# Crossbar transposes on the SP queue, staged row loads from POOL, and paired scores in a fused mLSTM and MLP kernel

## The chip, the cores and the metric

One core of one Trainium2 chip. The metric is the device time of one execution in microseconds (us). Medians are over several executions; each execution is also listed with its span (first to last instruction, some 1.7 us less than the time) and with the mean clock that TensorE was granted. Engines are named as in the profile: PE (TensorE), ACT (ScalarE), DVE (VectorE), POOL (GpSimd), SP (the queue that issues DMAs, "SPq"). PSUM is the memory that PE writes its results to. A crossbar transposition is a DMA issued with `transpose=True`; a DMA lands when the semaphore that tells of its end is raised.

## The reference, cut to what matters

```python
# attention part: q, k, v, o_gate: (4, 8, 768, 40); i_gate, f_gate: (4, 8, 768)
for t in range(S):
    m_new = maximum(f[t] + m, i[t]);  f_stab = exp(f[t] + m - m_new);  i_stab = exp(i[t] - m_new)
    C = f_stab * C + i_stab * outer(v[t], k[t]);   n = f_stab * n + i_stab * k[t]
    y[t] = sigmoid(o[t]) * (C @ q[t]) / maximum(abs(n . q[t]), 1)
x = y.transpose(0, 2, 1, 3).reshape(3072, 320)
# MLP part
h = x @ w_in                               # 320 -> 2048
out = (0.5 * (h + sqrt(h * h + 4))) @ w_out  # 2048 -> 320
```

The kernel uses that the input gates decide the state after the first 64 rows: only the first 128 rows of a batch need scores against k; all later rows multiply q with one 40x41 state per head. A flag is computed on the chip, and a general path runs if the assumption fails.

## The kernel before

The 3072 rows are 12 blocks of 256. A block passes: q cast and padded (POOL), q transposed, numerators (PE), division (DVE), gating `xt = y * sigmoid(o)` (POOL), x transposed, and then the MLP in four **units** of 512 hidden columns: 12 first-stage matmuls on PE, a square and a root on ACT, an addition on DVE. 48 units in all; the second stage follows in 48 half sums of 8 matmuls each, and 24 output tiles are copied and stored. In the traces of this case every engine works through its instructions in the order in which the program issues them (run 1 shows a wait of 5.70 us that comes of it); tables decide, in half slots of a unit, where each attention step is put between the units.

```python
STEPS = {                      # block: half slot of each step
    ...
    4: dict(pr=17, q_=24, n0=25, n1=26, x=29),          # pr: casts on POOL, q_: transpose q
    5: dict(pr=20, k_=23, q_=28, s0=28, s1=29, n0=31, n1=34, x=36),   # s: scores, n: numerators
    ... }
SECOND = (0, 0, 0, 0, 0, 0, 1, 1, 2, ...)      # second-stage halves issued in each slot
XT = (3, 7, 8, 9, 10)                          # x copies that ACT makes; DVE makes the others

def evacuate(on_act, n, dst, src):             # PSUM to SBUF
    if n in on_act: nc.scalar.activation(out=dst, in_=src, func=AF.Copy)
    else:           nc.vector.tensor_copy(out=dst, in_=src)

def s_q(blk, tag):                             # s_x is the same on xt; s_k: eight, on kh
    tp = psum([128, 2, G3, 128], BF, tag, "tp")      # tag "at": one PSUM tile for all these steps
    for t in range(2):
        for g in range(G3):
            nc.tensor.transpose(tp[:, t, g, :], qb[blk % 2][:, t, g, :], ident)
    evacuate(QT, blk, qT, tp)

def s_sc(b, half, tag):                        # one matmul per head, 128x128, k padded to 128
    for n in range(4):
        h = half * 4 + n
        nc.tensor.matmul(out=sp[:, n, :], lhsT=kT[:, h, :], rhs=qT[:, t, h // 3, :], ...)

def load_rows():                               # all three later batches at one point, from SP
    for b in range(1, B): ...
        nc.sync.dma_start(...)
def store(blk, ts, op):
    evacuate(OUT, blk * 2 + ts, osb, op)
    nc.sync.dma_start(out=dst, in_=osb)        # at once
```

Of the kernel before, what the change touches and what calls it, by code (L numbers as in the profile page):

```python
# [17 lines left out]
STEPS = {  # L18
    1: dict(pr=None, q_=0, n0=2, n1=3, x=6),
    2: dict(pr=8, k_=7, q_=9, s0=10, s1=11, n0=12, n1=13, x=15),  # L20
    3: dict(pr=14, g=16, q_=17, n0=17, n1=19, x=20),
    4: dict(pr=17, q_=24, n0=25, n1=26, x=29),
    5: dict(pr=20, k_=23, q_=28, s0=28, s1=29, n0=31, n1=34, x=36),
    6: dict(pr=31, g=38, q_=35, n0=43, n1=40, x=46),
    7: dict(pr=36, q_=39, n0=47, n1=48, x=53),
    8: dict(pr=37, k_=44, q_=50, s0=52, s1=55, n0=54, n1=56, x=61),
    9: dict(pr=54, g=57, q_=59, n0=60, n1=63, x=67),
    10: dict(pr=51, q_=65, n0=65, n1=68, x=75),
    11: dict(pr=64, k_=70, q_=71, s0=72, s1=74, n0=82, n1=79, x=85),
}  # L30
SIGM = (15, 30, 56)
EARLY = (3, 6, 7, 16, 17, 18, 19, 24, 30, 37)
SECOND = (0, 0, 0, 0, 0, 0, 1, 1, 2, 2, 1, 1, 1, 1, 1, 1, 0, 2, 0, 1, 1, 0, 2, 1, 1, 1, 1, 1, 1, 1, 1, 2, 0, 1, 1, 1, 1, 1, 1, 0, 2, 0, 2, 1)
QT = (1, 2, 7)
XT = (3, 7, 8, 9, 10)
OUT = (2, 3, 4, 5, 6, 7, 8, 9, 13, 14, 15, 16, 17, 18, 19, 20)
ALONE = (6, 7, 12, 13, 18, 19, 24, 25, 26, 27, 30, 31, 36, 37, 42, 43)
CLEAR = 8
ROWS = 8
FLAGS = (59, 61, 80, 86)  # L40

# [146 lines left out]
def kernel(  # L188
# [14 lines left out]
    T = 128  # L203
# [31 lines left out]
    with tc.manual_schedule():  # L235
# [39 lines left out]
        def load_w_in(lo, hi):  # L275
            nc.gpsimd.dma_start(out=w_in[:, :, lo:hi], in_=moe_w_in[0:256, lo:hi].rearrange("(g p) n -> p g n", p=128))
            for i in range(2):
# [22 lines left out]
        nc.gpsimd.memset(caus, 1.0)  # L300
        nc.gpsimd.affine_select(out=caus, in_=caus, compare_op=ALU.is_ge, fill=0.0, base=0,
                                pattern=[[1, 128]], channel_multiplier=-1)

# [4 lines left out]
        vwb = [const.tile([128, H, D + 1], BF, name=f"vw{i}") for i in range(2)]  # L308
        kTb = [const.tile([128, H, 128], BF, name=f"kT{i}") for i in range(2)]
        nc.vector.memset(kb[0], 0.0)  # L310
        nc.vector.memset(vwb[0], 0.0)
        nc.vector.memset(kh, 0.0)
        nc.vector.memset(kTb[0][:, :, TK:128], 0.0)
        for i in range(2):
# [21 lines left out]
        def psum(shape, dt, tag, name):  # L336
            return ps.tile(shape, dt, tag=tag, name=name, bufs=3 if tag == "hp" else 1)
# [18 lines left out]
        def vcast(b, eng):  # L356

            vw = vwb[b % 2]
            wb = wE[0:TK, 0, b * H:(b + 1) * H].unsqueeze(2)
            eng.tensor_copy(out=vw[0:TK, :, D:D + 1], in_=wb)  # L360
            eng.tensor_tensor(out=vw[0:TK, :, 0:D], in0=vf[b], in1=wb.to_broadcast([TK, H, D]), op=ALU.mult)
            state[b, "vw"] = vw

        def qcast(blk, eng, ts=(0, 1)):
# [18 lines left out]
        def evacuate(on_act, n, dst, src):  # L383
            if n in on_act:
                nc.scalar.activation(out=dst, in_=src, func=AF.Copy)  # L385
            else:
                nc.vector.tensor_copy(out=dst, in_=src)  # L387

        def s_q(blk, tag):
            tp = psum([128, 2, G3, 128], BF, tag, "tp")  # L390
            for t in range(2):
                for g in range(G3):
                    nc.tensor.transpose(tp[:, t, g, :], qb[blk % 2][:, t, g, :], ident)  # L393
            qT = work.tile([128, 2, G3, 128], BF, tag="qT", name="qT")
            evacuate(QT, blk, qT, tp)
            state[blk, "qT"] = qT

        def s_k(b, tag):
            kp = psum([128, H, 128], BF, tag, "kp")
            for h in range(H):  # L400
                nc.tensor.transpose(kp[:, h, :], kh[:, h, :], ident)
            kT = kTb[b % 2]
            nc.vector.tensor_copy(out=kT[:, :, 0:TK], in_=kp[:, :, 0:TK])
            state[b, "kT"] = kT

# [10 lines left out]

        def s_sc(b, half, tag):
            blk, t = b * 3 + 2, PAIRS[2].index(0)
            sp = psum([128, 4, 128], FP, tag, "sp")
            kT, qT = state[b, "kT"], state[blk, "qT"]  # L420
            for n in range(4):
                h = half * 4 + n
                nc.tensor.matmul(out=sp[:, n, :], lhsT=kT[:, h, :], rhs=qT[:, t, h // 3, :], start=True, stop=True)  # L423
            if half == 0:
                state[b, "scm"] = work.tile([128, H, 128], BF, tag="scm", name="scm")
            nc.vector.tensor_tensor(out=state[b, "scm"][:, half * 4:half * 4 + 4, :], in0=sp,  # L426
                                    in1=caus.unsqueeze(1).to_broadcast([128, 4, 128]), op=ALU.mult)

        def s_num(blk, t, tag, peng=nc.gpsimd):
            b, tt = blk // 3, PAIRS[blk % 3][t]  # L430
            np_ = psum([128, H, D + 1], FP, tag, "np")
            if tt == 0:
                for h in range(H):
                    nc.tensor.matmul(out=np_[:, h, :], lhsT=state[b, "scm"][:, h, :], rhs=state[b, "vw"][:, h, :],
                                     start=True, stop=True)
            else:
                for g in range(G3):
                    n = min(3, H - 3 * g)
                    nc.tensor.matmul(out=np_[:, 3 * g:3 * g + n, :], lhsT=state[blk, "qT"][:, t, g, :],  # L439
                                     rhs=state[b, "gm"][:, 3 * g:3 * g + n, :], start=True, stop=True)  # L440
# [16 lines left out]

        def s_x(blk, tag):
            xp = psum([128, 2, G3, 128], BF, tag, "xp")
            for t in range(2):  # L460
# [17 lines left out]
        gates_T("at")  # L478
        vcast(0, nc.vector)
        idle(9)  # L480
        s_g(0, "hp")


        qcast(0, nc.vector, (0,))
        for o, i in zip(padded(qb[0][:, 1]), heads(tile_of(ql, 0, 2))):
            nc.scalar.activation(out=o, in_=i, func=AF.Copy)
        idle(8)
        tp = psum([128, 2, 1024], BF, "hp", "tp")
        np_ = psum([128, 2 * H, 64], FP, "hp", "np")
        qT = work.tile([128, 2, G3, 128], BF, tag="qT", name="qT")  # L490
        for t in range(2):
            for g in range(G3):
                nc.tensor.transpose(tp[:, t, g * 128:(g + 1) * 128], qb[0][:, t, g, :], ident)
        nc.vector.tensor_copy(out=qT[:, 0], in_=tp[:, 0, 0:384].rearrange("p (g n) -> p g n", g=G3))
        nc.scalar.activation(out=qT[:, 1], in_=tp[:, 1, 0:384].rearrange("p (g n) -> p g n", g=G3), func=AF.Copy)
        sigm(0, 1, 3)
# [21 lines left out]
        nc.scalar.activation(out=tiny[:, 0:1], in_=tiny[:, 1:2], func=AF.Sqrt)  # L518
        def load_rows():
            for b in range(1, B):  # L520
                if b == 1:

                    kf[b] = res.tile([TK, H, D], FP, name=f"kf{b}")
                    nc.vector.memset(kf[b][0:1, 0, 0:1], 0.0)
                    nc.sync.dma_start(out=kf[b], in_=k[b, :, 0:TK, :].rearrange("h s d -> s h d"))
                else:
                    chunk(kf, "kf", k, b)
                chunk(vf, "vf", v, b)
                later(ql, "ql", q, b, 1, NTL)
                later(ol, "ol", o_gate, b, 1, NTL)  # L530
                chunk(q0, "q0", q, b)
                chunk(o0, "o0", o_gate, b)
                if b == 1:
                    for n in range(2):
                        nc.sync.dma_start(out=fi[:, n, T:S], in_=gates[n][:, T:S])

# [28 lines left out]

        khcast(0, nc.gpsimd)


# [5 lines left out]
        def put(hs, f, *a):  # L574

            bank = () if f in (sigm, load_rows, flag1, flag2, flag3) else ("op" if hs <= 10 and hs % 2 == 0 else "at",)
            plan.setdefault(hs, []).append(lambda: f(*a, *bank))
# [26 lines left out]

        for m in (kb[1], vwb[1], kTb[1][:, :, TK:128]):
            pre.setdefault(CLEAR, []).append(lambda m=m: nc.gpsimd.memset(m, 0.0))
        for blk, row in STEPS.items():
            put_block(blk, **row)
        put(ROWS, load_rows)
        for b, hs in enumerate(SIGM):  # L610
# [8 lines left out]
        def flush():  # L619
            while adds:  # L620
                adds.pop(0)()

        def store(blk, ts, op):
            b, tt = blk // 3, PAIRS[blk % 3][ts]
# [4 lines left out]
            else:  # L629
                dst = out[b * S + T:(b + 1) * S, :].rearrange("(p j) d -> p j d", j=NJ)[:, tt - 1, :]  # L630
            nc.sync.dma_start(out=dst, in_=osb)

# [15 lines left out]

        def at(table, hs):
            for f in table.get(hs, ()):  # L650
                f()
# [62 lines left out]
        for u in range(3):  # L714
            first(blk, (u,))
            adds.append(unit(blk, u))
            while len(todo) > 4:
                mm2_part(todo.pop(0))
            flush()
        mm2_part(todo.pop(0), "at")  # L720
        mm2_part(todo.pop(0), "at")
# [3 lines left out]
        mm2_part(todo.pop(0))  # L725
        mm2_part(todo.pop(0))
        tc.mark_branch_hint_location("general", "LikelyTaken")
        mm2(blk, 0, list(range(NF)), "at")
        mm2(blk, 1, list(range(NF)), "op")
    short.close()  # L730

# [33 lines left out]
```

## Time and profile before

| | before |
|---|---|
| median of the executions | 159.7 us |
| span of the profiled one, clock | 158.5 us, 0.995 |
| PE, ACT, DVE, POOL busy | 141.2, 128.9, 106.7, 60.3 us |

The prediction shows the main rows and reads them. I use the start of a unit's square on ACT as a mark, since every kernel here has the same 48. These are busy times of the engines (us, and number of instructions) between the marks of units 0, 8, 16 and 47 in the kernel before; the columns are stretch, length, PE, PE's weight loads, DVE, ACT, POOL, clock, DMA share, GB/s:

```profile
0.00:15.08 15.08, 10.83 (x105) 8.67 (x106) 8.89 (x36) 7.69 (x12) 13.86 (x27) 1.00 0.92 187
15.08:38.93 23.85, 20.14 (x201) 13.78 (x200) 16.65 (x30) 20.58 (x21) 12.13 (x33) 1.00 0.95 189
38.93:62.79 23.86, 21.72 (x215) 15.80 (x212) 16.46 (x30) 22.54 (x26) 8.66 (x23) 1.00 0.77 207
62.79:146.75 83.96, 81.93 (x782) 58.24 (x781) 61.51 (x101) 76.05 (x85) 25.65 (x60) 1.00 0.09 31
```

From unit 0 to 8 no compute engine is full, from 8 to 16 ACT nearly is (22.5 of 23.9), from 16 to 47 PE is (81.9 of 84.0).

### The profile page before, as it was taken

To read this page: it belongs to the slowest core of one execution; us is meant where nothing else is said; L and a number is where in the kernel's file an instruction comes from. 1 tells how busy PE (TensorE), PEld (TensorE's weight loads), DVE (VectorE), ACT (ScalarE), POOL (GpSimd) and SP (SyncE) were. 2 spreads that over 40 slices of the span, in tenths; PEclk is the share of its full clock that TensorE was granted. 3 is DMA by queue.
4 is the path that set the end of the run, shared out by engine and by line. 5 is a ranking of instruction groups with operands and counts; after the bars stand their busy time and mean duration, and the time that the engine had idled before them with its cause. 6 is when DMAs were issued, how large, how long until landed. Compare 5 with 4: busy or idle time off the path is not lost.

```text
span 158.5 us, 3472 instructions
## 1 busy us (share of the span) xinstructions
PE 141.2 (89%) x1343; PEld 101.0 (64%) x1343; DVE 106.7 (67%) x199; ACT 128.9 (81%) x144; POOL 60.3 (38%) x142
## 2 busy tenths in 40 slices
PE   5787686989899979999999999898999999999960
PEld 5665455657667666767766766676767777666740
DVE  5655687794666858696868787987775586655520
ACT  3656999768999799999968879999979999889500
POOL 7999390282270560740507722337220022000000
PEclk9999999999999999999999999999999999999997
DMA  3999995996989930110110010011011011101121
GB/s 56 258 241 192 186 225 81 288 227 123 348 149 296 286 134 0 41 41 4 41 41 24 22 41 31 15 43 41 4 41 41 4 43 41 41 6 41 43 91 43
DMA packets 26389, 15.54 MB, mean 98 GB/s; under 512 B 13360, under 2 KB 25760, under 8 KB 26368
## 3 DMA queue, kind: packets, MB, share of 16 engines
q1 hardware_dynamic: 21376, 11.18, 25.2%
q0 software_dynamic: 3936, 3.93, 14.1%
q10 hardware_dynamic: 1056, 0.16, 0.6%
q8 instruction: 11, 0.18, 0.5%
q14 instruction: 10, 0.08, 0.2%
HBM read 13.96 MB, written 3.93 MB: 113 GB/s over the span
## 4 chain that ended last, share of the span: by engine, by line
PE 73%; DVE 12%; ACT 4%; issue 3%; POOL 3%; DMA 1%; SPq 0%; DVEq 0%; POOLq 0%; ACTq 0%
PE op L640 30%; PE hp L665 23%; PE hp L672 7%; PE xp L462 3%; DVE gt L686 3%; POOL xt L456 3%; PE np L439 2%; PE sp L423 2%; DVE qT L387 2%; PE tp L393 2%; DMA fi<-in_i_gate_dram 1%; DVE xT L387 1%; ACT t L685 1%; ACT t L684 1%; PE warm L472 1%
## 5 line engine op out<-in xcount | busy, mean ns | idle before, releaser
L686 DVE SCALAR_TENSOR_TENSOR gt<-hp,t 128x1024 bf16<-128x1024 f32 x48 | 58.3, 1220 | 18.5 <-ACT t L685 16.8
L640 PE MATMUL op<-w_out,gt 128*128 128x320 bf16 x384 | 57.7, 299 | 0.2 <-ACT osb L385 0.2
L684 ACT ACTIVATE t<-hp 128x1024 f32<-128x1024 f32 x48 | 48.8, 1016 | 10.0 <-PE hp L672 7.1
L685 ACT ACTIVATE t<-t 128x1024 f32<-128x1024 f32 x48 | 50.7, 1057 | 1.5
L456 POOL TENSOR_TENSOR xt<-y,sig 128x320 bf16<-128x320 f32 (+1 forms) x44 | 25.1, 593 | 69.8 <-DVE y L452 45.8
L665 PE MATMUL hp<-xT,w_in 128*128 128x256 bf16 x384 | 49.9, 273 | 1.4 <-DVE xT L387 1.2
L640 PEld LDWEIGHTS <-gt 128*128 128x128 bf16 x384 | 35.7, 98 | 13.8 <-issue 1.6
L665 PEld LDWEIGHTS <-w_in 128*128 128x128 bf16 x384 | 35.2, 98 | 8.9 <-issue 5.1
L672 PE MATMUL hp<-xT,w_in 64*128 64x256 bf16 x192 | 17.1, 273 | 0.1
L672 PEld LDWEIGHTS <-w_in 64*128 64x128 bf16 x192 | 6.4, 94 | 8.3 <-issue 7.7
L452 DVE SCALAR_TENSOR_TENSOR y<-den,np 128x320 f32<-128x320 f32 x18 | 8.8, 488 | 1.5
L370 POOL CAST qb<-ql 128x240 bf16<-128x240 f32 (+1 forms) x32 | 8.9, 316 | 0.4 <-POOL xt L456 0.3
L462 PE MATMUL xp<-ident,xt 128*128 128x128 bf16 x72 | 7.1, 220 | 2.0 <-DVE xt L512 1.0
L472 PE MATMUL warm<-ident 128*128 128x128 bf16 x68 | 7.1, 278 | 1.4 <-POOL identF L267 1.4
L385 ACT ACTIVATE osb<-op 128x320 f32<-128x320 f32 x16 | 6.8, 423 | 1.8 <-PE op L640 1.8
L439 PE MATMUL np<-gm,qT 128*128 128x123 bf16 (+1 forms) x54 | 5.5, 214 | 2.7 <-DVE qT L387 1.4
L462 PEld LDWEIGHTS <-xt 128*128 128x128 bf16 x72 | 4.8, 97 | 4.8 <-POOL xt L456 1.4
L426 DVE TENSOR_TENSOR scm<-sp,caus 128x512 bf16<-128x512 f32 x8 | 5.4, 688 | 3.3 <-PE sp L423 3.3
L443 DVE TENSOR_REDUCE den<-np 128x8 f32<-128x8 f32 x22 | 3.5, 161 | 5.5 <-PE np L439 4.2
L439 PEld LDWEIGHTS <-qT 128*128 128x128 bf16 x54 | 3.7, 98 | 5.2 <-DVE qT L387 1.7
L472 PEld LDWEIGHTS <-ident 128*128 128x128 bf16 x68 | 6.0, 130 | 1.5 <-POOL identF L267 1.4
L381 ACT ACTIVATE sig<-ol 128x1600 f32<-128x1600 f32 (+2 forms) x5 | 6.3, 1259 | 0.6 <-DMA ol<-in_o_gate_dram 0.6
(102 smaller groups left out, 114.7 us busy)
## 6 DMA issues: line engine op xcount, KB each, us to landing
out_dram<-osb SPq DMA_DIRECT2D x24, 160.0 KB, 1.8
ql<-in_q_dram SPq DMA_DIRECT2D x3, 800.0 KB, 5.2
ol<-in_o_gate_dram SPq DMA_DIRECT2D x3, 800.0 KB, 7.0
w_out<-in_moe_w_out_dram POOLq DMA_DIRECT2D x2, 640.0 KB, 11.4
w_in<-in_moe_w_in_dram POOLq DMA_DIRECT2D x2, 256.0 KB, 5.4
w_in<-in_moe_w_in_dram POOLq DMA_DIRECT2D x1, 512.0 KB, 7.7
ol<-in_o_gate_dram POOLq DMA_DIRECT2D x1, 480.0 KB, 5.4
q<-in_q_dram SPq DMA_DIRECT2D x3, 160.0 KB, 7.2
```

Of the source, the lines that this page charges most:

```text
L370: eng.tensor_copy(out=o, in_=i)
L439: nc.tensor.matmul(out=np_[:, 3 * g:3 * g + n, :], lhsT=state[blk, "qT"][:, t, g, :], rhs=state[b, "gm"][:, 3 * g:3 * g + n, :], start=Tru ...
L452: nc.vector.scalar_tensor_tensor(out=y1, in0=den.to_broadcast([128, H, D]), scalar=1.0, in1=np_[:, :, 0:D], op0=ALU.min, op1=ALU.mult)
L456: peng.tensor_tensor(out=o, in0=y[:, lo:DM], in1=s[:, lo:DM], op=ALU.mult)
L462: nc.tensor.transpose(xp[:, t, g, :], xt[blk % 2][:, t, g * 128:(g + 1) * 128], ident)
L472: nc.tensor.matmul(out=warm[:, 0:128], lhsT=ident, rhs=ident, start=True, stop=True)
L640: nc.tensor.matmul(out=op, lhsT=gts[blk][:, ff, ts * 128:(ts + 1) * 128], rhs=w_out[:, ff, :], start=(ff == 0), stop=(ff == NF - 1))
L665: nc.tensor.matmul(out=hps[blk, u][:, f, :], lhsT=w_in[:, g, ff * 128:(ff + 1) * 128], rhs=xT[:, :, g, :], start=start and g == 0 and f % ...
L672: nc.tensor.matmul(out=hps[blk, u][:, 2 * i + f, :], lhsT=w_in3[p, (2 * u + f) * 128:(2 * u + f + 1) * 128], rhs=xT[p, :, 2, :], start=sta ...
L684: nc.scalar.activation(out=t1, in_=hp, func=AF.Square, scale=0.5)
L685: nc.scalar.activation(out=t1, in_=t1, func=AF.Sqrt, bias=1.0)
L686: return lambda: nc.vector.scalar_tensor_tensor(out=gts[blk][:, u * UF:(u + 1) * UF, :], in0=hp, scalar=0.5, in1=t1, op0=ALU.mult, op1=ALU ...
```

## The change

Its intent is to take transpositions, their PSUM tiles and their copies off PE, ACT and DVE. For that, the SP queue must be free: loads go to POOL in three bursts, and stores are issued two half slots late. Scores of two heads share a matmul. All tables were set anew. At the start, block 0's transpositions get two PSUM tiles, and the cast of its first tile moves in front of the state step. The core of the diff:

```diff
-    5: dict(pr=20, k_=23, q_=28, s0=28, s1=29, n0=31, n1=34, x=36),
+    5: dict(pr=19, k_=19, q_=22, s0=25, s1=26, n0=28, n1=30, x=34),
 ... (all rows of STEPS, SIGM, EARLY, SECOND, QT, XT, OUT, ALONE, FLAGS)
+QDMA = (2, 3, 5, 6, 7, 8, 9, 10, 11)
+XDMA = (3, 4, 5, 7, 8, 9, 10, 11)
-ROWS = 8
+ROWS = (11, 23, 41)
 def s_q(blk, tag):
+    if blk in QDMA:
+        crossbar(qT..., qb[blk % 2]...)       # nc.sync.dma_start(..., transpose=True)
+        return
 def s_x(blk, tag):
+    if blk in XDMA:
+        crossbar(xT..., xt[blk % 2]...); return
-    for h in range(H): nc.tensor.transpose(kp[:, h, :], kh[:, h, :], ident)
-    nc.vector.tensor_copy(out=kT[:, :, 0:TK], in_=kp[:, :, 0:TK])
+    crossbar(kTb[b % 2], kh[0:TK]...)
+    nc.sync.dma_start(out=vpb[b % 2][TK:128, :, 1, :], in_=vwb[b % 2][0:TK, 1:H:3, :])
 def s_sc(b, half, tag):
-    for n in range(4): ...                    # 8 matmuls a batch
+    hs = ((0, 2, 3), (5, 6))[half]            # 5 a batch, lhsT = k of two heads
-def load_rows(): ... nc.sync
+def load_row(b): ... nc.gpsimd                # put in front of the steps at half slot ROWS[b - 1]
-    nc.sync.dma_start(out=dst, in_=osb)
+    stores.append((now[0], dst, osb))         # sent two half slots later
-tp = psum([128, 2, 1024], BF, "hp", "tp")     # block 0
+tp = [psum([128, 384], BF, "hp", "tp") for t in range(2)]
```

## The prediction

> **What bounds the kernel now.** I read the busy rows and the slices of the page first, then the granted clock and the busy times by stage, then the groups, the waits, and last the chain of waits to see what one transposition costs on TensorE where it counts.
>
> ```profile
> PE 141.2 (89%) x1343; PEld 101.0 (64%) x1343; DVE 106.7 (67%) x199; ACT 128.9 (81%) x144; POOL 60.3 (38%) x142
> PE   5787686989899979999999999898999999999960
> ACT  3656999768999799999968879999979999889500
> DMA  3999995996989930110110010011011011101121
> ```
>
> TensorE (PE) is nearly full from the second fifth of the span to the last slice but one; ScalarE (ACT) is close behind; the DMA engines are full only for the first 15 slices (59 us). The same by stage (columns: stretch, its length, busy us of each engine, clock, DMA share, GB/s):
>
> ```profile
> 13.70:36.90 23.20, 19.49 (x198) 13.21 (x198) 17.06 (x32) 18.78 (x19) 13.51 (x35) 1.00 0.98 196
> 36.90:60.00 23.10, 20.96 (x202) 15.27 (x200) 14.57 (x26) 21.56 (x24) 8.66 (x23) 1.00 0.86 222
> 60.00:80.00 20.00, 19.85 (x200) 14.52 (x198) 15.83 (x27) 19.31 (x22) 7.34 (x19) 1.00 0.07 25
> 80.00:100.00 20.00, 19.51 (x190) 13.86 (x189) 15.35 (x28) 16.78 (x18) 8.07 (x20) 1.00 0.10 34
> 100.00:120.00 20.00, 18.69 (x183) 13.16 (x182) 16.41 (x28) 18.53 (x21) 7.95 (x17) 1.00 0.08 26
> 120.00:140.00 20.00, 19.92 (x188) 14.20 (x186) 13.02 (x22) 17.90 (x22) 2.29 (x4) 1.00 0.10 35
> ```
>
> Three regimes. Up to about 37 us nobody is full except the DMA engines (0.98): loads and short dependent chains set the pace. From 37 to 60 us ACT (21.6 of 23.1) and PE (21.0) both nearly bound it. From 60 to 147 us PE is busy 85.0 of 87 us (the four rows and 7.0 of the next 7): there a microsecond of PE work taken away should be a microsecond of time. The clock is 1.00 throughout, so it is no lever. In the timeline of PE after 13.7 us I count 7.9 us of idle time; these entries of the list of waits are the ones behind a transposition and its copy out of PSUM:
>
> ```profile
> PE np L439 <- DVE qT L387: 1.4, 2, 0.7
> PE sp L423 <- ACT qT L385: 1.2, 1, 1.2
> PE sp L423 <- DVE qT L387: 0.6, 1, 0.6
> PE sp L423 <- DVE xT L387: 0.6, 1, 0.6
> ```
>
> Together 3.9 us. The last one is telling: a score matmul waits for the copy of an unrelated x transposition, because transpositions, scores, numerators and state all take turns in the one PSUM tile tagged "at". What one group costs where PE is the chain (start, us on the chain, what):
>
> ```profile
> 48.15 0.45 PE kp L401 x8
> ...
> 56.41 0.35 PE tp L393 x6
> 56.78 0.57 DVE qT L387
> 57.39 0.38 PE sp L423 x4
> ...
> 58.86 0.35 PE xp L462 x6
> 59.23 0.57 DVE xT L387
> ```
>
> Six q or x transpositions occupy PE for 0.35 us and eight k transpositions for 0.45 us, although the groups call each of them 219 ns: they are pipelined at 57 ns. So the chain, not the groups' means, gives the price.
>
> **What the Trainium skill says.** "VectorE: DVE Perf Modes", section "The three transpose paths": the crossbar takes 1309 ns for a 128x128 bf16 block against 390 ns on TensorE, but lands in SBUF rather than PSUM, so no copy follows it. This trace has no crossbar transposition; the TensorE figure is for one alone, and here it is 219 ns long and 57 ns apart. "TensorE: Matmul & The Clock Gate", section "Part 4: PE-mode transpose", says that a copy out of PSUM has to follow; the trace agrees (0.56 us on DVE, 0.79 on ACT per block). "DMA: Bandwidth & Descriptors", section "Latency and other measured facts", gives 261 GB/s for a DMA transposition in one kernel; its section "Anatomy of one DMA — SWDGE (gpsimd) path" a fixed 2.0 us per DMA, mostly the receipt. The trace agrees on the second in kind: a 160 KB store lands 1.8 us after its issue. An estimate from these pages for one 128x768 bf16 block (196,608 bytes): 2.0 + 0.75 = 2.8 us if it streams, 6 x 1.31 = 7.9 us if six blocks go one after another.
>
> **The change, part by part.**
>
> *PE work removed.* q by crossbar in 9 blocks: 9 x 0.35 = 3.15 us. x in 8 blocks: 8 x 0.35 = 2.8. k in all 4 batches: 4 x 0.45 = 1.8. Scores go from 8 matmuls per batch to 5: 12 fewer at about 57 ns (same 128 columns as a transposition) = 0.7. The numerators of the first tile go from 8 to 5; eight take 0.20 us on the chain, so about 0.3 in all. Sum 8.7 us of PE.
>
> *Evacuations.* ACT loses q of blocks 2 and 7 (2 x 0.79), x of blocks 3, 7, 8, 9, 10 (5 x 0.79) and, by the new list, 7 output copies (16 to 9, 0.42 each): 8.5 us less. DVE loses 7 q copies (0.56), 3 x copies (0.56), 4 k copies (0.42) and 3/8 of the masking (5.4 us becomes 3.4 by columns): 9.3 us less, and takes 7 output copies at 0.49, so 5.9 us less net. Both sides of the second-tightest engine are relieved in about PE's proportion: over 15 to 147 us ACT is busy 119.4 and PE 124.1 of 132; they become 111 and 115.5. That is why I don't expect ACT to become the bound.
>
> *Waits removed.* Four of the PE waits above go with their transpositions, 3.9 us at most; and the shared PSUM tile has 21 fewer tenants.
>
> *Added: 21 crossbar transpositions and 3 or 4 small moves on the SP queue.* They are off all compute engines. They cost only if the result comes later than its reader. The schedule leaves, between the cast of q and its first use, some 5 half slots in most blocks (pr 19 to s0 25, 28 to 34, 52 to 59), and between x and the first matmul 3 to 9. A half slot is 132 us / 88 = 1.5 us or a bit less, so there are about 4 to 8 us, against the estimate of 2.8 to 7.9. Mostly hidden. Stores are issued two half slots late so that a store not yet ready doesn't hold a transposition up in the same in-order queue (SP waited 87 us on output copies before).
>
> *Added on POOL: 20 load issues.* POOL's issues take 0.95 us each in this trace (rows of ql, q and o from POOL: 954, 969, 949 ns), 19 us in all, in bursts of 8, 6 and 6 (7.6, 5.7, 5.7 us). POOL goes from 60 to about 80 us of busy time, not a bound, but a burst sits in front of the gating products xt, each pair of which takes 1.2 us on POOL and lies on the path to the next block's x.
>
> *Start.* The two q transpositions of block 0 get a PSUM tile each, so that ACT need not wait for DVE's copy before its own (8.69 to 9.06, then 9.08 to 9.58): about 0.4 us.
>
> *Sum by regime.* From 60 us on: 6 q groups (2.1), 5 x groups (1.75), 2 k groups (0.9), scores and numerators of two batches (0.5) = 5.3 us, and about 1.2 us of the waits: 6.5. From 37 to 60 us: PE falls by about 2.2 and its waits by 2.0, but ACT, at 21.6 of 23.1, falls only by one x copy and up to two output copies, 1.2 to 1.6, so I take 1.8. Before 37 us: 0.4 from the start; what else goes there (q of 2, k of 0, the 1.2 us wait for ACT) is not on PE's bound, and the POOL burst is a charge against it: net 0.4. Sum 8.7 us less. For new waits on crossbars or POOL I take 0.6 back: 8.1 less, so 159.8 - 8.1 = **151.7 us**.
>
> **The rivals.**
>
> *The crossbar takes the wait's place.* If a transposition needs nearer 8 us, or SP spends microseconds in issuing each and serialises 21 of them with 24 stores, PE stops at scores, numerators and first matmuls. For it: the block figure of 1309 ns, and that in the first 60 us the DMA engines are loaded anyway, so that a 160 KB load took 7.2 us and more to land. Against it: after 60 us they are busy 7 to 10%, the q and x gaps were evidently widened, and q of block 4 and x of block 6 are kept on PE, near the second and third burst of loads. If each of 17 transpositions left 0.4 us of wait, the time would be some 158; if only the first few do, 153.5.
>
> *POOL becomes the bound in the second stage.* The burst at half slot 11 (7.6 us) and the cast of block 3, which needs rows of that same burst, stand in program order before the gating of block 2. In the kernel before, that gating ran at 30.2 to 33.3 us and the first matmuls of block 2 at 34.2. If POOL starts the burst at 24 us (after its casts), it ends at 31.6, and if the cast then waits for the rows to land, block 2 comes 3 to 5 us later. For it: POOL is in order. Against it: ACT in the kernel before didn't start block 2's squares before 38.9 anyway, since it stood in the sigmoid of the next batch, so most of the delay would be hidden. Worst case 155.5.
>
> *More than the sum.* With the PSUM tile free, all 7.9 us of PE idle time shrink, and the loads spread over three stages relieve the first 60 us: 148.
>
> **Range and chances.** The PE sum is firm (counts and chain prices); what is not is the first 60 us and the latency of the crossbar. The crossbar rival at its full size I hold for 1 in 12, the POOL one at 3 us or more for 1 in 5, the better one for 1 in 6. That gives 148.0 to 155.8 us as a range for 8 times in 10. Faster by over 2% means below 156.6: 0.91. Within 2%: 0.07. Slower: 0.02.
>
> **What would show it.** In the changed profile: PE busy near 132 to 133 us and no group of k transpositions; ACT near 120, DVE near 101, POOL near 80; from 60 us to the tail PE still busy 96% or more; crossbar issues landing in 3 to 5 us; no wait of a first matmul or a numerator on a DMA above 0.5 us. The prediction is wrong if PE's busy time falls by 8 us and its idle time grows by as much, with a DMA or POOL's xt as releaser, or if the block 2 matmuls start after 38 us and ACT does not make up for it.

## The result, and the profile after

| | before | changed |
|---|---|---|
| median | 159.7 us (159.59 to 159.95) | 154.59 us (154.07 to 156.14) |
| ratio, 95% interval | 1 | 0.9694 (0.962 to 0.977) |
| span of the profiled execution | 158.5 us | 152.4 us |
| PE, ACT, DVE, POOL busy | 141.2, 128.9, 106.7, 60.3 | 132.8, 121.7, 100.8, 77.4 |

Ratios are the mean time of one kernel's fast runs over that of the other's of the same rounds, so not quite the ratio of the medians. The change is faster by 3.1%. Its four executions, with their clocks, are 154.07 (0.996), 154.18 (0.995), 155.01 (0.989) and 156.14 us (0.978): they scatter with the clock, which those of the kernel before (0.99 to 1.00) don't. More on that below. The spans differ by 6.1 us and the medians by 5.1: the profiled execution of the kernel before took 160.26 us, 0.56 more than its median, so about half a microsecond of what the stages below show is that execution's.

The page of the changed kernel, with the rows that the prediction showed of the one before:

```profile
PE 132.8 (87%) x1185; PEld 93.3 (61%) x1185; DVE 100.8 (66%) x190; ACT 121.7 (80%) x130; POOL 77.4 (51%) x168
PE   6697679747999995899999899899999999999970
ACT  3648959938999779999997568999979989699610
DMA  2999999999037699503799150132333103101111
```

PE's busy time fell by 8.4 us, but the span by 6.1: PE has new idle time. The row of PE shows weaker slices in the first quarter (7, 4, 7 in the eighth to tenth, where it had 9, 8, 9), and the DMA row three load hills instead of one. The busy times between the same marks (units 0, 8, 16, 47):

```profile
0.00:14.27 14.27, 10.84 (x103) 9.49 (x103) 7.81 (x32) 7.69 (x13) 12.85 (x26) 1.00 0.91 185
14.27:39.95 25.68, 18.74 (x171) 12.04 (x171) 16.19 (x32) 20.42 (x22) 19.92 (x46) 1.00 1.09 202
39.95:63.61 23.66, 21.91 (x205) 15.36 (x204) 16.91 (x31) 21.30 (x23) 17.13 (x38) 1.00 0.71 174
63.61:140.88 77.27, 74.76 (x665) 51.94 (x663) 57.52 (x95) 69.29 (x72) 27.47 (x59) 1.00 0.36 88
```

| stretch | before | changed | difference |
|---|---|---|---|
| start to unit 0 | 15.08 | 14.27 | -0.81 |
| unit 0 to 8 | 23.85 | 25.68 | +1.83 |
| unit 8 to 16 | 23.86 | 23.66 | -0.20 |
| unit 16 to 47 | 83.96 | 77.27 | -6.69 |
| unit 47 to the end | 11.75 | 11.52 | -0.23 |

(A DMA share above 1, as in the second row, is how the profile prints it; I take it only as a sign that the engines are loaded.)

So the gain is all in the PE-bound stretch (PE's busy time there fell by 7.2, the stretch by 6.7), the middle gave nothing, and the beginning lost more than twice what the new start had won.

What became of the middle shows in the chain of waits of the changed kernel, here the part before block 4's first matmul, unit 16 (start, us on the chain, what):

```profile
48.08 1.15 POOL xt L475 x2
49.23 0.67 POOL kf L243
49.91 0.68 POOL vf L243
50.59 0.87 POOL ql L248
51.48 0.90 POOL ol L248
52.38 0.87 POOL q L243
53.25 0.87 POOL o L243
54.14 1.14 POOL xt L475 x2
55.30 5.72 DMA xT<-xt
61.07 1.05 PE hp L695 x8
```

POOL gates the first tile of block 4, issues the second burst of loads (4.9 us), and only then gates the second tile; the crossbar then needs 5.7 us to land, in the burst's traffic. PE stood 1.69 us. In the same way 0.78 us were lost before the scores at 84 us (timeline of PE; in brackets the idle time before it and what ended it):

```profile
61.07 1.05 PE L695 MATMUL hp<-xT,w_in 128*128 128x256 bf16 x8 [1.69 <-DMA xT<-xt]
...
84.36 0.33 PE L438 MATMUL sp<-qT,kT 128*128 128x128 bf16 x3 [0.78 <-DMA qT<-qb]
```

The issues of the transpositions (number, median us from issue to landing):

```profile
qT<-qb SPq DMA_TRANSPOSE x9, 3.2
...
xT<-xt SPq DMA_TRANSPOSE x8, 2.5
...
kT<-kh SPq DMA_TRANSPOSE x4, 4.7
```

Taken one by one, 11 of the 21 land in 2.5 or 2.6 us; the slow ones are 4.0 to 7.4 us (one 3.2), nearly all while weights or rows are being loaded (5.0 and 5.6 at 24 and 32 us, 5.7 at 55, 6.9 and 5.3 at 76 and 79). Two slow ones have no load in flight: 4.5 at 61 and 4.0 at 107.

### The profile page after: what moved, and what is told of

The parts are those of the page before. It is cut to its first block, busy times and chain, and to the rows that moved or that the text cites. A ratio compares the mean times of both kernels' runs of the same rounds, so it can differ in the third digit from the quotient of the medians.

```text
span 152.4 us, 3186 instructions
## 1 busy us (share of the span) xinstructions
PE 132.8 (87%) x1185; PEld 93.3 (61%) x1185; DVE 100.8 (66%) x190; ACT 121.7 (80%) x130; POOL 77.4 (51%) x168
## 4 chain that ended last, share of the span: by engine, by line
PE 52%; DVE 16%; DMA 10%; ACT 8%; POOL 5%; issue 4%; SPq 0%; DVEq 0%; POOLq 0%; ACTq 0%
PE op L668 24%; PE hp L695 16%; PE hp L702 5%; DVE gt L716 5%; ACT t L714 5%; DMA xT<-xt 4%; DMA qT<-qb 3%; ACT t L715 3%; POOL xt L475 2%; PE np L458 2%; DVE y L471 2%; PE warm L496 2%; DVE osb L396 2%; DMA fi<-in_i_gate_dram 1%; DMA out_dram<-osb 1%
## 5 line engine op out<-in xcount | busy, mean ns | idle before, releaser
L695 PEld LDWEIGHTS <-w_in 128*128 128x128 bf16 x384 | 35.9, 98 | 11.2 <-issue 4.1
L702 PE MATMUL hp<-xT,w_in 64*128 64x256 bf16 x192 | 18.0, 274 | 0.0
L396 DVE COPY osb<-op 128x320 f32<-128x320 f32 x15 | 7.3, 486 | 9.6 <-PE op L668 6.3
L496 PE MATMUL warm<-ident 128*128 128x128 bf16 x68 | 7.8, 297 | 1.4 <-POOL identF L269 1.4
L496 PEld LDWEIGHTS <-ident 128*128 128x128 bf16 x68 | 6.7, 140 | 1.5 <-POOL identF L269 1.4
L442 DVE TENSOR_TENSOR scm<-sp,caus 128x384 bf16<-128x384 f32 (+1 forms) x8 | 3.9, 488 | 3.6 <-PE sp L438 3.6
L394 ACT ACTIVATE osb<-op 128x320 f32<-128x320 f32 x9 | 3.8, 424 | 1.9 <-PE op L668 1.9
L248 POOL DMA_DIRECT2D ql<-in_q_dram x5 | 4.5, 907 | 0.5 <-DMA w_in<-in_moe_w_in_dram 0.5
```

Of the source, the lines that this page charges most:

```text
L496: nc.tensor.matmul(out=warm[:, 0:128], lhsT=ident, rhs=ident, start=True, stop=True)
L695: nc.tensor.matmul(out=hps[blk, u][:, f, :], lhsT=w_in[:, g, ff * 128:(ff + 1) * 128], rhs=xT[:, :, g, :], start=start and g == 0 and f % ...
L702: nc.tensor.matmul(out=hps[blk, u][:, 2 * i + f, :], lhsT=w_in3[p, (2 * u + f) * 128:(2 * u + f + 1) * 128], rhs=xT[p, :, 2, :], start=sta ...
```

## The experiments

All gave correct results. "Unit 8" and the like is the start of that unit's square. Two theories stood at first: the gain comes only where PE is the bound, so early crossbars can go back to PE for nothing; and either POOL's bursts or the crossbar's landing under load cost the middle. The rival: PE work counts everywhere.

**1. Early crossbars back on PE.**

```diff
-QDMA = (2, 3, 5, 6, 7, 8, 9, 10, 11)      -XDMA = (3, 4, 5, 7, 8, 9, 10, 11)
+QDMA = (6, 7, 8, 9, 10, 11)               +XDMA = (7, 8, 9, 10, 11)
```

> The changed kernel with q of blocks 2, 3, 5 and x of blocks 3, 4, 5 transposed on TensorE again (6 groups, 6 x 0.35 = 2.1 us of PE work put back before about 61 us). Theory (the gain comes only from the PE-bound stretch after some 70 us; earlier, PE's work is worth nothing and the crossbar's landing of 5 to 6 us under the loads costs): 153.5 to 154.8, the changed kernel's 154.6 or up to 1 us less, and no first matmul waiting on a crossbar near 61 us. Rival (PE work counts everywhere): 154.6 + 2.1 = 156.7.

Measured: 173.73 us (172.47 to 174.11), ratio 1.083. Both theories miss by far: six groups of 0.35 us cost 19 us. The timeline of PE, then that of ACT, show how:

```profile
46.48 0.51 PE L486 MATMUL xp<-ident,xt 128*128 128x128 bf16 x3 [0.53 <-POOL xt L475]
49.57 0.49 PE L411 MATMUL tp<-ident,qb 128*128 128x128 bf16 x6 [2.58 <-ACT xT L394]
49.90 4.01 PE L668 MATMUL op<-w_out,gt 128*128 128x320 bf16 x16
...
82.28 0.43 PE L458 MATMUL np<-gm,qT 128*128 128x123 bf16 x3 [5.70 <-ACT xT L394]
82.51 4.47 PE L668 MATMUL op<-w_out,gt 128*128 128x320 bf16 x16
```

```profile
46.71 1.02 ACT L714 ACTIVATE t<-hp 128x1024 f32<-128x1024 f32 x1 [0.57 <-DVE gt L716]
47.76 1.06 ACT L715 ACTIVATE t<-t 128x1024 f32<-128x1024 f32 x1
48.73 0.79 ACT L394 ACTIVATE xT<-xp 128x768 bf16<-128x768 bf16 x1
```

PE transposes x, but the copy stands in ACT's queue behind a square and a root (at 82 us behind two units and a table load), and the next user of the one PSUM tile "at" must wait for it: 2.58 and 5.70 us. Behind that user stand all other matmuls, since PE keeps its order. And after such a pause the clock is low: 16 second-stage matmuls take 4.01 and 4.47 us instead of 2.33. Over the run PE idles 9.5 us more after unit 0 than in the changed kernel, and 17 us (from 33.3, 50.4 and 81.1 us on) run at half clock. The stretches around the second pause show it (seventh and following columns: POOL busy, clock, DMA share, GB/s):

```profile
76.00:82.20 6.20, 0.49 (x6) 0.37 (x6) 1.16 (x2) 6.14 (x7) 0.00 (x0) 0.91 0.00 0
82.20:88.00 5.80, 5.72 (x26) 3.56 (x26) 1.84 (x5) 0.03 (x1) 1.14 (x2) 0.51 0.00 0
88.00:92.00 4.00, 4.00 (x42) 2.74 (x40) 3.51 (x6) 2.87 (x3) 1.94 (x4) 1.00 0.34 90
```

So in the new tables a transposition on PE costs not its 0.35 us but the waits at both of its ends. The crossbar takes those waits out of PE's queue into SP's; the new tables are built on that. "Undo a part" is therefore not a clean price of that part, which I had not thought of.

**2. No crossbar for q and x at all.**

```diff
+QDMA = ()
+XDMA = ()
```

> The changed kernel with no crossbar transposition of q or x at all (17 groups back on TensorE, 5.95 us of PE work), k still by crossbar, scores still in pairs. Theory: only the 11 groups after 61 us cost, 11 x 0.35 = 3.85 us and up to 1 us of waits for their copies, less what the early ones give back: 157.5 to 159.5. Rival (PE work counts everywhere): 160.5 or more, no better than the kernel before. Second rival (the gain is in the k part, the pairs and the output copies' move): under 156.

Measured: 188.51 us (186.57 to 189.52), ratio 1.172: a miss for the same reason, and more of it (29 us of idle PE from unit 0 to 47, against 11).

**3. The row loads from SP again, in three bursts.**

```diff
-ROWS = (11, 23, 41)      # load_row: nc.gpsimd, in front of the steps of that half slot
+ROWS = (12, 23, 41)      # load_row: nc.sync, behind them
```

> The changed kernel with the three bursts of row loads issued by SP instead of POOL, at the same places but the first one half slot later (behind the crossbar of q of block 2). Traffic the same, POOL 17 us less busy. Theory A (the POOL bursts stand in front of the gating products and cost about 1.5 us in the first 61 us): 152.5 to 153.8, and the gating of block 4's second tile at about 50.5 instead of 54.1 us. Theory B (it is the crossbar's landing under the traffic, whoever issues it): 154 to 155. Rival C: the issues on SP (0.6 us each, longer under load) now hold up the crossbars: above 155.

Measured: 161.04 us (160.33 to 163.47), ratio 1.005; clock 0.94 to 0.96 in every execution; the profiled one (163.47) is slow, so I take only the order of events from it. This run doesn't decide what it was made for. On SP the first burst had a store ahead of it that was not ready before 31.9 us, so it started at 32.4 instead of 23.6, and POOL waited 9.8 us for k's rows. What follows is only that SP's order counts: here the loads stood behind a late store.

**4. x of block 4 alone on PE.**

```diff
-XDMA = (3, 4, 5, 7, 8, 9, 10, 11)
+XDMA = (3, 5, 7, 8, 9, 10, 11)
```

> The changed kernel with x of block 4 alone transposed on TensorE. Its crossbar took 5.7 us to land under the second burst of loads, and the first matmul at 61.1 us waited 1.7 us for it. Theory B (the landing under load costs): the wait goes, PE pays 0.35 us: 153.2 to 153.9 if it is carried to the end, and the units after block 5's start come about 1.2 us earlier. Rival (what is gained there is lost to ACT or to the next wait before 70 us): 154.3 to 154.8.

Measured: 160.0 us (157.59 to 160.6), ratio 0.9996, fast executions at clocks of 0.973 to 0.995, three of six slow; the profiled one is 157.59 at 0.995. Units up to 13 stand within 0.5 us of the changed kernel's; unit 14 is 3.8 us later, and 3.4 of it stay to the last unit. PE now itself waits for the gating behind the burst:

```profile
53.41 0.34 PE L486 MATMUL xp<-ident,xt 128*128 128x128 bf16 x3
55.58 0.50 PE L486 MATMUL xp<-ident,xt 128*128 128x128 bf16 x3 [1.82 <-POOL xt L475]
56.73 0.27 PE L438 MATMUL sp<-qT,kT 128*128 128x128 bf16 x2 [0.65 <-DVE xT L396]
```

1.82 + 0.65 us of waits for 0.35 of work. With the crossbar, PE had used that time for other matmuls. Neither expectation held; the same lesson as run 1, at the price of one group. It also shows that a delay in the middle is carried to the end nearly whole: there is no slack later to swallow it. (The expectations of runs 4 and 7 call unit 16, the first of block 4, block 5's start.)

**5. One part alone, in the kernel before: late crossbars.** Crossbars for q of blocks 6 to 11 and x of 7 to 11, with delayed stores, and everything else, tables included, as before (q of four blocks issued up to 3 half slots earlier).

```diff
 before.py
+QDMA = (6, 7, 8, 9, 10, 11)
+XDMA = (7, 8, 9, 10, 11)
-    nc.sync.dma_start(out=dst, in_=osb)
+    stores.append((now[0], dst, osb))
-    10: dict(pr=51, q_=65, ...     +    10: dict(pr=51, q_=62, ...    # and blocks 8, 9, 11
```

> The kernel before with one part of the change: q of blocks 6 to 11 and x of blocks 7 to 11 by crossbar (issued up to 3 half slots earlier than TensorE did them), stores issued two half slots late so that they don't stand before the crossbars. Loads, k, scores and the rest of the schedule as before. 11 groups leave TensorE, 11 x 0.35 = 3.85 us, all after 70 us. Theory (in the PE-bound stretch PE work comes off the time one for one, even without any retuning): 160.0 - 3.9 = 156.1, within 0.8. Rival (without the retuned positions the crossbars' 2.5 us land too late and new waits eat it): 158 or more. Other rival (waits for copies go as well): 155 or less.

Measured: 156.95 us (156.48 to 157.33), ratio 0.9805, clock 0.994 to 1.00. The expected 156.1 within 0.8 is missed by 0.05 us; against the 2% line the verdict is unclear, though the interval lies below 1. The marks say more: from unit 16 to 47 the stretch fell from 83.96 to 80.91 us, 3.05 us, where 3.85 of PE work had been worked out and 4.0 of PE's busy time went; units 2 to 19, which it doesn't touch, stood 0.4 to 0.7 us later than in the kernel before's profile. So where PE is the bound, whole groups (matmuls, their copies and their waits; the late stores are in the edit too) come off at about four fifths of the price of their PE work, without new tables. The matmuls alone were not isolated.

**6. The changed kernel with the old tables.**

```diff
-STEPS, SIGM, EARLY, SECOND, ALONE of the changed kernel
+the same of the kernel before
```

> The changed kernel with the schedule tables of the kernel before (where each step stands, which units are paired or flushed early, how many second-stage halves stand in each slot); crossbars, row loads on POOL in bursts at 11, 23 and 41, pairs, and the choice of engine for the copies as in the changed kernel. Theory (the positions were retuned because a crossbar takes its step off PE's queue, so the gain needs both): between the two, 156 to 159.5. Rival (the change's mechanisms do it alone): 154 to 155. Other rival (the first experiments show how brittle the tables are): over 162.

Measured: 175.31 us (172.27 to 175.88), ratio 1.099; the rival that the tables are brittle is right. The profile is of an execution listed as slow (174.93; the fast ones took 172.27 and 174.12). In it PE waits on the crossbars themselves (PE waits: us in total, times, longest):

```profile
PE sp L438 <- DMA qT<-qb: 11.0, 3, 4.4
```

The three waits stand at 24, 60 and 127 us. The old tables leave none to two half slots between q's transposition and the scores; a copy by DVE needed 0.6 us, a crossbar 2.5 at least. So neither the mechanisms nor the tables alone are the change: with these crossbars, early and late, the tables must move, and with the tables moved the crossbars must stay.

**7. The second burst half a slot later**, behind the gating of block 4.

```diff
-ROWS = (11, 23, 41)
+ROWS = (11, 24, 41)
```

> The changed kernel with the second burst of row loads one half slot later, behind the gating of block 4's second tile instead of in front of it. The burst kept that gating from about 50 to 54.1 us, and x of block 4 by crossbar then took 5.7 us and PE stood 1.7 us at 61 us. Theory (the burst in front of the gating costs): the 1.7 us wait goes, units from block 5 on come 1 to 1.7 us earlier, and that is carried to the end: 153 to 153.6. Rival (the crossbar now lies wholly under the burst's traffic and lands as late, or block 6's rows come too late): 154.3 or more.

Measured: 157.54 us (156.48 to 158.32), ratio 0.9854 (unclear against the 2% line): the rival. The wait at 61 us is gone, but now q of block 6 is late, whose rows come with that burst (timeline of PE):

```profile
65.91 0.46 PE L458 MATMUL np<-gm,qT 128*128 128x123 bf16 x3 [2.69 <-DMA qT<-qb]
```

Units from 16 on are 3.0 to 3.3 us later. The wait moved, and grew.

**8. The first eight units as before**, with q of block 2 on PE; loads on POOL and k by crossbar stay.

```diff
-    1: dict(pr=None, q_=1, n0=3, n1=3, x=4),
-    2: dict(pr=9, k_=1, q_=11, s0=12, s1=13, n0=13, n1=13, x=15),
+    1: dict(pr=None, q_=0, n0=2, n1=3, x=6),
+    2: dict(pr=8, k_=1, q_=9, s0=10, s1=11, n0=12, n1=13, x=15),
-QDMA = (2, 3, 5, ...            +QDMA = (3, 5, ...
 EARLY, ALONE, SECOND of slots 0 to 7 as before; one second-stage half moved from slot 5 to 8
```

> The changed kernel with the first eight units as in the kernel before: steps of blocks 1 and 2 at the old places, q of block 2 transposed on TensorE (its crossbar took 5.0 us to land under the loads), old pairing and order there; one second-stage half moved from slot 5 to slot 8. Theory (the early loss, 0.8 us ahead at the first unit and 1.5 us behind at unit 7, is the schedule's and the slow crossbar's): unit 7 comes 1.5 to 2.3 us earlier and the whole 153.0 +- 0.6. Rival (it is POOL's first burst): unit 7 about as late, 154.5 or more.

Measured: 153.19 us (152.99 to 153.51), ratio 0.9584 (0.9553 to 0.9614), as expected. Unit 7 stands 2.4 us earlier, unit 8 2.0, and units from 16 on 1.1. Part of the early win went back between units 8 and 10, where PE is now the pace: that is where I had put the moved half (1.09 us). POOL's first burst is in it, so it was not what the beginning had lost to.

How the loss divides between the steps' places and the slow crossbar of q of block 2 the marks say in part. Run 8 is ahead of the changed kernel by 1.87 us at unit 3 and 1.20 at unit 5 (27.16 us there), before that crossbar had landed (28.72). So at least 1.2 of the 2.0 us are not the crossbar's. One wait there is that of block 1's two numerator steps, which the new table puts into one half slot and so into one PSUM tile; the scores of block 2 come after the crossbar has landed, and PE does not wait for it (changed kernel):

```profile
18.52 0.32 PE L458 MATMUL np<-gm,qT 128*128 128x123 bf16 x3 [1.07 <-DVE y L471]
...
29.53 0.34 PE L438 MATMUL sp<-qT,kT 128*128 128x128 bf16 x3
31.02 0.27 PE L438 MATMUL sp<-qT,kT 128*128 128x128 bf16 x2 [1.15 <-DVE scm L442]
31.81 0.31 PE L458 MATMUL np<-gm,qT 128*128 128x123 bf16 x3 [0.52 <-DVE scm L442]
33.14 0.21 PE L454 MATMUL np<-vp,scm 128*128 128x82 bf16 x1 [1.02 <-DVE y L471]
```

The crossbar still sets how early the scores could be: in run 8 they start at 26.11. All four executions are at clocks of 0.995 to 1.00.

**9 to 11. Three repairs on top of run 8**: (9) the second burst split, the four light loads at half slot 20, when POOL is idle, the two heavy ones at 24; (10) the moved half put into slot 6; (11) both, and the third burst at 34 instead of 41.

```diff
 run 9:   ROWS[1] = 23  ->  k, v, q0, o0 at 20; later q, later o_gate at 24
 run 10:  SECOND = (0, 0, 0, 0, 0, 0, 1, 1, 2, ...  ->  (0, 0, 0, 0, 0, 0, 2, 1, 1, ...
 run 11:  both, and ROWS = (11, ..., 34)
```

> The version with the old first eight units (153.2), with the second burst cut in two: the four light loads (k, v and the first tiles of q and o, 480 KB) one step earlier, where POOL stood idle from 43.4 to 47.0 us, the two heavy ones (1.6 MB) behind the gating of block 4's second tile. Theory (POOL's burst in front of that gating caused the 1.6 us wait at 60 us): gating at about 49.5 instead of 53.1, the wait gone, units from 16 on 1.3 to 1.6 us earlier, 151.6 to 152.0. Rival (the heavy traffic, now starting later, makes the crossbar of x of block 4 or the rows of block 6 late): 153 or more, with a wait on a crossbar between 58 and 68 us.

> The same version (153.2), only the second-stage half that I had moved from slot 5 to slot 8 put into slot 6, where PE waits anyway. Theory (that half is the 1.0 us which that version lost between units 8 and 10, where PE is the bound): units from 10 on 0.9 to 1.1 us earlier, 152.1 to 152.4. Rival (PE in slot 6 pushes the scores and gating of block 2 back): 153 or more.

> Both of these, and the third burst moved from half slot 41 to 34, into POOL's idle 4 us, so that k and q of block 8 are cast and transposed before its traffic (their crossbars took 6.9 and 5.3 us to land and the scores at 83 us waited 0.8 us). If all three are separate terms: 153.2 - 1.5 - 1.0 - 0.7 = 150.0, within 0.5. Rival (the burst now makes the crossbar of q of block 7, issued at about 66 us and wanted at 72, late): 151 or more and a wait on a crossbar near 70 us.

Run 9: 156.51 us (154.58 to 157.49), ratio 0.9731. The gating of block 4 comes at 49.1 and the wait on its x is gone, but q of block 5, whose crossbar is issued at 45.5 us, now lands 7.3 us later. The 480 KB of light loads are in flight with it (k's takes 5.7 us to land, in run 8 2.6; the last lands at 52.9, like the crossbar), and from 50.2 us a heavy load and the next crossbar, so how much each adds isn't taken apart. In run 8 it had landed after 3.1 us:

```profile
52.97 0.33 PE L439 MATMUL sp<-qT,kT 128*128 128x128 bf16 x3 [2.68 <-DMA qT<-qb]
```

After it, the clock, in three stretches of 3.41 us (same columns as above):

```profile
50.96:54.37 3.41, 1.40 (x15) 1.00 (x15) 0.56 (x1) 0.29 (x1) 2.68 (x7) 1.00 0.94 263
54.37:57.79 3.42, 3.42 (x19) 2.10 (x16) 1.22 (x3) 2.08 (x2) 1.12 (x4) 0.50 1.01 324
57.79:61.20 3.41, 3.41 (x35) 2.16 (x33) 2.82 (x5) 2.08 (x2) 1.14 (x2) 1.00 0.41 108
```

A pause of 2.7 us is followed by 3.4 us at half the clock; PE is "busy" throughout, but runs 19 matmuls where the next stretch has 35. So the wait costs twice: units 16 and on are 3.9 us late for 2.7 us of wait.

Run 10: median 154.04 us (152.45 to 155.13), ratio 0.9669. The profiled execution (152.45, clock 1.00) has units from 16 on 0.6 to 0.75 us earlier than run 8, where 0.9 to 1.1 were expected; two other fast ones were at clocks of 0.981 and 0.989 and took 154.19 and 153.88, the fourth (155.13) is slow. As a time this is no improvement that I can show.

Run 11: median 155.84 us (153.43 to 157.61); half of its executions are slow, and no ratio is given. The two fast ones, 153.43 and 154.95, are above what was expected. Its profile has the wait of run 9 (2.63 us at 53 us); the third burst's early place works: the scores at 83 us no longer wait. But no low clock follows the wait:

```profile
48.03:51.44 3.41, 2.22 (x18) 1.23 (x16) 2.10 (x5) 3.25 (x4) 2.23 (x5) 1.00 1.01 88
51.44:54.85 3.41, 1.62 (x18) 1.16 (x19) 0.56 (x1) 0.05 (x1) 2.40 (x6) 1.00 1.09 286
```

The two runs differ in where these stretches begin and end. In every trace here the half clock lasts 3.41 or 6.83 us at a time (less at the very end), and all its stretches in one trace begin on one grid of 3.41 us; the edges above are on the grids of runs 9 and 11. What tells the two apart is the idle time of PE within one stretch of the grid: 2.01 us in run 9, at most 1.79 in run 11, where an edge cuts the same pause in two. Over the 14 traces, from 8 us on and without the tails, all 14 stretches at full clock with 1.90 us or more of idle PE were followed by half clock, 2 of 9 with 1.65 to 1.82, and none with less.

**12. Run 11, with q of block 5 on PE and its scores half a slot later.**

```diff
-QDMA = (3, 5, 6, ...      +QDMA = (3, 6, ...
-    5: dict(..., q_=22, s0=25, s1=26, ...      +    5: dict(..., q_=24, s0=26, s1=27, ...
```

> The version of the last run with all three edits, with q of block 5 on TensorE (its crossbar took 7.3 us to land beside the light loads and PE stood 2.6 us at 53 us): q at half slot 24, the scores one half slot later. Theory (what costs in the middle stage is a crossbar landing beside loads, not POOL's issues): the 2.6 us wait goes, x of block 4 (6.1 us to land) is there in time because its gating is no longer behind the burst, and no PE wait on a crossbar is left between 45 and 85 us: executions at clock 1.00 take 150.5 to 151.3, and all of them 150.5 to 152.5. Rival (the copies and the shared PSUM tile take the wait's place, as in the first experiments): over 153.

Measured: 153.07 us (152.09 to 154.82), ratio 0.9544 (0.9504 to 0.9585); clocks 0.982 to 1.00, two of six executions slow. In its profile the two waits on crossbars at 53 and 60 us are gone, one of 0.48 us is left at 73 us, and another stands where block 4 begins:

```profile
60.78 0.39 PE L710 MATMUL hp<-xT,w_in 64*128 64x256 bf16 x4 [1.21 <-DVE gt L724]
```

PE waits for a free hp tile. The stretch from unit 8 to 16, which holds a table load, the sigmoid of a batch and eight units on ACT, shows why repairs here give little:

```profile
38.62:62.52 23.90, 22.42 (x210) 15.88 (x210) 17.63 (x33) 21.25 (x24) 18.29 (x40) 1.00 0.66 164
```

23.90 us against 23.86 in the kernel before and 23.66 in the changed one, with ACT busy 21.3 and PE 22.4. The theory of the crossbar beside loads is right for the waits it named; the time it was to free is taken by the next wait in line.

The marks of the kernels that the argument uses (us; executions at clocks of 0.995 to 1.00):

| | unit 0 | unit 8 | unit 16 | unit 47 | median time |
|---|---|---|---|---|---|
| before | 15.08 | 38.93 | 62.79 | 146.75 | 159.7 |
| changed | 14.27 | 39.95 | 63.61 | 140.88 | 154.6 |
| run 5, late crossbars alone | 14.80 | 39.30 | 63.17 | 144.08 | 156.95 |
| run 8, old first eight units | 14.14 | 37.91 | 62.49 | 139.75 | 153.2 |
| run 10 | 14.27 | 38.23 | 61.91 | 139.00 | 154.0 |
| run 12 | 14.33 | 38.62 | 62.52 | 139.25 | 153.1 |

Runs 8 and 12 beat both kernels, and both intervals lie below the changed kernel's. Run 8 is the one to keep: the two intervals overlap, and only run 8 has all its executions at clocks of 0.995 to 1.00.

## Why the prediction was right or wrong

The range and the class held. The size did not: 8.1 us were forecast, 5.1 came in the medians and 6.1 in the spans. By its own steps:

**PE work removed: right.** 8.7 us forecast, 8.4 measured, from the prices on the chain. (The four waits in the prediction's list add to 3.8 us, not 3.9; they are gone from the changed profile, but with the new ones PE's idle time from unit 0 to 47 rose from 7.9 to 11.2 us.) The evacuations too: DVE fell by 5.9, exactly as worked out; ACT's copies fell by 8.6 us in the groups, though its busy time only by 7.2, since neighbouring instructions overlap in part. POOL came to 77.4 instead of 80, mostly because the issues of k, v and the gates take only 0.5 to 0.7 us.

**From 60 us on: right.** 6.5 us forecast, 6.69 measured from unit 16 to 47. Run 5 shows that this stretch pays for groups taken off PE without the rest of the change, 3.05 us for 3.85 us of PE work.

**From 37 to 60 us: the term that failed first.** Forecast -1.8, measured -0.20. I let ACT's lost copies count as time. They were taken off (ACT's busy time there fell from 22.54 to 21.30), but the stretch stayed. What took their place was POOL's burst in front of the gating of block 4 and the crossbar that landed in its traffic. The prediction had named both rivals and set 0.6 us for them; the one wait at 61 us is 1.7. Runs 7, 9 and 12 each removed that wait and got another in its place, so how much of the -1.8 was to be had at all stays open; the stretch was 23.66 us or more in every kernel whose stretch I give.

**Before 37 us: the term with the wrong sign.** Forecast -0.4, measured +1.0 at unit 8. The start did more than forecast (-0.81 for -0.4); the diff also moves block 0's first cast forward, which the prediction doesn't count and no run isolates. But the new steps of blocks 1 and 2 lost 1.83. Run 8 undid them and got 2.0 back, with the POOL burst left in. So the suspicion I had put down as the charge here, POOL's burst, was the wrong one. "What else goes there is not on PE's bound" missed that the new places of the steps could cost: the marks under run 8 put 1.2 us or more of the loss into units 1 to 5, before q of block 2 had landed. What the crossbar of that q, 5.0 us to land while the DMA engines were full, adds to it is not shown.

**The crossbar's landing: right and incomplete.** 2.8 us as the low estimate, 2.5 measured with quiet queues. "Mostly hidden" holds for the 11 quiet ones. Beside loads it is up to 7.4, near the high estimate, but for another reason: other transfers, not six blocks in series.

**The clock: missing from it.** I wrote that the clock is no lever. Two of the changed kernel's four executions had 0.989 and 0.978 and took 0.9 and 2.0 us more than the other two's mean. In runs 1 and 9 the trace shows the clock fall to 0.5 for 3.4 or 6.8 us after a pause of PE of 2.6 to 5.7 us. The changed kernel's slower executions were not traced. In its profile the longest pause is 1.69 us and the clock stays whole, but the three waits at 31 to 33 us (shown under run 8) add to 2.69 us within 3.4. Counted back from the half clock of its tail, which begins at 150.75 us, the grid has an edge at 31.29 us, between them; an execution whose grid falls otherwise would have them in one stretch. Two slower executions in four fit that, and so does run 8, with at most 1.85 us in any 3.41 us, and no slower one in four; it isn't proof. Runs 10 and 12 have at most 1.56 and 1.80 in their profiles and executions at 0.98 all the same. About 0.5 us of the 3 us missing in the median is the clock (154.59 against 154.12, the mean of the two at full clock).

**What I did not foresee at all** is what the crossbar buys: not 0.35 us of PE, but that PE no longer stands in its own queue for POOL's gating before a transposition and for ACT's copy after it. Runs 1, 2 and 4 show it, against all their expectations: with the new tables, one group back on PE costs 3.4 us in the profiled execution at full clock (5.4 in the medians, most of its executions having a lower clock), six cost 19, part of it through the half clock.

## What to carry to other kernels

Moving an operation from an in-order engine to a DMA moves its two waits as well, and a schedule tuned on top of that can no longer be priced by putting the operation back: price a part by adding it alone to the kernel before. Put a crossbar where no bulk load is in flight, or leave it the time to land beside one (here up to 7.4 us instead of 2.5). Look at idle time in sums over a few microseconds, too: several short pauses close together can cost clock. Read the difference stage by stage with marks that both kernels have: the total hid a gain of 6.7 and a loss of 1.8.

## What the Trainium skill lacked or had wrong

- "VectorE: DVE Perf Modes", section "The three transpose paths": 1309 ns for a 128x128 crossbar transposition is no guide for a larger one; a 128x768 (six blocks) landed 2.5 us after its issue on quiet queues, and held SP for 1.2 us.
- "DMA: Bandwidth & Descriptors", section "Rules for kernel authors", says that a transposition next to ordinary DMAs needs nothing. That is about correctness; no page says what it costs in time: 4.0 to 7.4 us to land beside loads of weights or rows, against 2.5 without them; 7.3 in run 9, where only 480 KB were ahead of it.
- "TensorE: Matmul & The Clock Gate", section "Part 4: PE-mode transpose", gives some 275 ns in a kernel's context; here 219 ns each, and 57 ns apart when six follow one another, which is what the chain pays. What its copy costs the next user of the PSUM tile (up to 5.7 us in run 1) is on no page I read.
- The same page, section "Why this matters for your kernels", asks for no pause of PE above about 3 us. Pauses of 2.58 and 2.68 us (runs 1 and 9) were followed by half clock; one of 2.63 in run 11's profile was not. In these traces the idle time within one stretch of the 3.41 us grid tells them apart: 1.90 us or more were followed by half clock 14 times of 14.
- "DMA: Bandwidth & Descriptors", section "Issuing engines are not separate DMA queues", calls the issue time usually small beside the DMA itself. That holds for one (0.7 to 0.9 us on POOL, 2.6 to 7.7 to land), but six in a row were 4.9 us and stood on the chain.
